# V loads of the eighteen late attention groups: from SyncE's queue to GpSimd's, in a planned attention and MLP kernel

## The chip, the cores and the metric

One core of a Trainium2 chip runs the program. The metric is the device time of one execution in microseconds, less is better. Engines are named as in the profile: PE is TensorE (PEld its weight loads), DVE VectorE, ACT ScalarE, POOL GpSimd, SP SyncE.

## What is computed

The reference is chunked attention with a few memory rows, then two MLPs in a row, all in float32:

```python
for c in range(nc):                      # 24 chunks of 32 queries; batch 4, heads 8, seq 768, head_dim 64
    q_c = q[:, :, c_start:c_end]
    k_full = np.concatenate([mem_k, k[:, :, l_start:r_end]], axis=2)   # 8 memory rows, 16 left, 32, 8 right
    v_full = np.concatenate([mem_v, v[:, :, l_start:r_end]], axis=2)
    scores = scale * np.matmul(q_c, k_full.transpose(0, 1, 3, 2))
    ...
    out[:, :, c_start:c_end] = np.matmul(a, v_full)                    # a: softmax of the scores
...
h = x @ w_in; g = s * np.maximum(h, 0) ** 2 + b; x = g @ w_out         # 3072 tokens, 512 -> 2048 -> 512
g = x @ w_gate; return (silu(g) * (x @ w_val)) @ w_out2                # 512 -> 1536 -> 512
```

## The kernel before

**Attention.** The 3072 queries are cut into 24 groups of 128 (four chunks, all eight heads), six groups to a batch. Three groups make a tile of 384 tokens, the unit of the first MLP. Groups 0 to 5 are called early (`EARLY`, L201): their work stands at the start of the program, and their queries and keys are turned by PE. Groups 6 to 23 are late: their work is spread among the first MLP's, and their queries and keys are loaded in blocks of 32 x 32 by `load_quadrant` (L312) into `qin` and `kin`, then turned by DVE: `turn_queries` writes `qt` (L355), `turn_keys` writes `kT` (L361). There is one `kin` and one `qt`, so the loads of a group can't start before `kT` of the group before it has been written. A late group has 36 such transfers, the first and the last of a batch 44. Below, K8 stands for the query and key transfers of group 8, kT8 and qt8 for its transposes, V8 for its values.

`load_values` (L377) fetches V of a group into one of two buffers by eight transfers, one for each chunk and half of the heads; at the ends of a sequence a chunk needs two pieces, and the first two groups of a batch load the memory rows too, and POOL copies these to the other three chunks (L391). So a group has 8, 10 or 12 transfers.

After the scores DVE takes the maximum (`mx`, L467), subtracts (`sc`, L480), sums (`rc`, L521, L524, L525) and, after the product with V, normalises (`on`, L530).

**First MLP.** Each weight pair (`load_w1`, L250; sixteen pairs, W0 to W15) is split by ACT and DVE into a high and a low part, so that three fast matmuls (L559, L560, L561) make one exact product; the last step of the split, L889, writes the low part. For a tile t and a slice m, `first_up` writes `hp` and `first_down` adds to `acc`. Between them DVE and ACT make `r`, its square, and the two parts `ghi` and `glo` (L612 or L610, L621 or L619). PE does the product up of the next slice before the product down of this one.

**Second MLP.** It begins at about 630 us and has no part in the change.

**What sets the order.** The program is not written in the order in which it runs. Every step is a task of a `Plan` (L63) with an engine, an estimated length, the tasks it depends on, and buffers that it takes and gives. `Plan.run` (L100) plays these tasks through in estimated time, always starting on a free engine the ready task with the longest way to the end, and the tasks are then emitted in the order in which they started there. PE's tasks are a fixed chain. DVE, ACT, POOL and SP each get one list, and on the chip each engine works through its list in order. A load is a task on SP, of 0.45 us per transfer, which needs one of two places called `fly`, followed by a task on MOVE, an engine that exists only in the plan:

```python
issue = issues[name] = plan.add(SP, 0.45 * n, emit, deps, [*get, "fly"], take=take)
return plan.add(MOVE, kilobytes / rate, None, [issue], put=["fly"], lag=1.8, give=give)
```

Of the kernel before, what the change touches and what calls it, by code (L numbers as in the profile page):

```python
# [146 lines left out]
def attention_and_two_mlps(  # L147
# [21 lines left out]
    nc = tc.nc  # L169
    B, H, S, D = q.shape  # L170
    NT, DM = out.shape
    NMEM = mem_k.shape[2]
# [7 lines left out]
    GB = S // GQ  # L180
    T = 3 * GQ
    NC = GQ // CHUNK
    WIN = LEFT + CHUNK + RIGHT
    KC = NMEM + WIN
# [16 lines left out]
    EARLY = 2 * GPB  # L201
# [110 lines left out]
    def load_quadrant(g, a, part):  # L312

        b, gi = divmod(g, GB)
        s0 = gi * GQ
        if a == 0 and part == 0:
            if "k" not in kept_in:
                kept_in["k"] = ld.tile([P, NP, KB, QUAD], F32, tag="kin", name="kin")
            loaded.setdefault(g, {})["q"] = ld.tile([P, NP, GQ // QUAD, QUAD], F32, tag="qin", name=f"qin{g}")
        e, half = divmod(a, 2)  # L320
        ds = slice(half * QUAD, (half + 1) * QUAD)
        qin, kin = loaded[g]["q"][a * QUAD:(a + 1) * QUAD], kept_in["k"][a * QUAD:(a + 1) * QUAD]

        def block(n, t, first, count):
            if count:
                nc.sync.dma_start(
                    out=kin[t:t + count, :, n], in_=k[b, e:H:2, first:first + count, ds].rearrange("j t i -> t j i")
                )

        at = s0 - LEFT  # L330
        left, over = max(0, -at), max(0, at + SPAN - S)
        whole = KB - 1 - (over > 0)
        if part == 0:
            if gi == 0:
                nc.sync.dma_start(out=kin[0:NMEM, :, 0], in_=mem_k[b, e:H:2, :, ds].rearrange("j t i -> t j i"))
            block(0, NMEM, 0, left)
            block(0, NMEM + left, at + left, QUAD - NMEM - left)
            if over:
                block(KB - 1, 0, S - QUAD + over, QUAD - over)
                block(KB - 1, QUAD - over, S - over, over)  # L340
            return
        for j in (2 * part - 2, 2 * part - 1):
            h = 2 * j + e
            first = at + QUAD - NMEM
            nc.sync.dma_start(
                out=kin[:, j, 1:1 + whole],
                in_=k[b, h, first:first + whole * QUAD, ds].rearrange("(n t) i -> t n i", t=QUAD),
            )
            nc.sync.dma_start(
                out=qin[:, j], in_=q[b, h, s0:s0 + GQ, ds].rearrange("(n t) i -> t n i", t=QUAD)  # L350
            )

    def turn_queries(g):
        staged[g] = {"qt": ap_.tile([P, NP, GQ], F32, tag="qt", name=f"qt{g}")}
        nc.vector.transpose(  # L355
            out=staged[g]["qt"].rearrange("p j s -> p (j s)"), in_=loaded[g]["q"].rearrange("p j n i -> p (j n i)")
        )

    def turn_keys(g):
        staged[g]["kT"] = t = ap_.tile([P, NP, KB * QUAD], F32, tag="kT", name=f"kT{g}")  # L360
        nc.vector.transpose(  # L361
            out=t.rearrange("p j s -> p (j s)"), in_=kept_in["k"].rearrange("p j n i -> p (j n i)")
        )

    def spread_keys(engine, g, mem):
        kT = staged[g]["kT"]
        if mem:
            copy(
                engine, staged[g]["kt"][:, :, :, 0:NMEM],
                kT[:, :, 0:NMEM].unsqueeze(2).to_broadcast([P, NP, NC, NMEM]),  # L370
            )
            return
        staged[g]["kt"] = kt = ap_.tile([P, NP, NC, KC], F32, tag="kt", name=f"kt{g}")
        w = kT[:, :, NMEM:KC]
        copy(engine, kt[:, :, :, NMEM:], bass.AP(tensor=w.tensor, offset=w.offset, ap=[w.ap[0], w.ap[1], [CHUNK, NC], [1, WIN]]))

    def load_values(g):  # L377

        b, gi = divmod(g, GB)
        s0 = gi * GQ  # L380
        n = g % 2
        if n not in v_bufs:
            v_bufs[n] = ld.tile([P, NC, NP, D], F32, tag=f"v{n}", name=f"v{n}")
        tv = v_bufs[n]
        for e in range(2):
            p0 = e * KC
            if gi < 2:
                mem = tv[p0:p0 + NMEM]
                nc.sync.dma_start(out=mem[:, 0], in_=mem_v[b, e:H:2].rearrange("h s d -> s h d"))
                for c in range(1, NC):  # L390
                    nc.gpsimd.tensor_copy(mem[:, c], mem[:, 0])  # L391
            for c in range(NC):
                a = s0 + c * CHUNK - LEFT
                left, over = max(0, -a), max(0, a + WIN - S)
                for row, first, n in (
                    (0, 0, left), (left, a + left, WIN - left - over), (WIN - over, S - over, over)
                ):
                    if n:
                        r0 = p0 + NMEM + row
                        nc.sync.dma_start(  # L400
                            out=tv[r0:r0 + n, c],
                            in_=v[b, e:H:2, first:first + n, :].rearrange("h s d -> s h d"),
                        )
        loaded.setdefault(g, {})["v"] = tv

    def bank(pool, tag, name):
# [2 lines left out]
    def stage_queries(g, early):  # L409
        tq = loaded[g]["q"]  # L410
        ps = bank(ps_acc, "acc2", f"psQ{g}") if early else bank(ps_a, "a", f"psQ{g}")
        qps = ps.rearrange("p (j s) -> p j s", j=NP)
        for j in range(NP):
            nc.tensor.transpose(qps[:, j, :], tq[:, j * P:(j + 1) * P], ident)
        staged[g] = {"q": qps}
# [370 lines left out]
    def second_store(h, s, i):  # L786
# [6 lines left out]
    ACT, DVE, PE, SP, MOVE = "ACT", "DVE", "PE", "SP", "MOVE"  # L793
    plan = Plan(
        dict(w=SLOTS - LENT, wt=SLOTS - 5, fly=2),
        dict(
            sc=LENT, f=2, own=1, qk=1, v=2, kT=1, kt=1, qt=1, at=1, on=1, x=2, r=4, ghi=2, glo=2, acc01=1,
            acc2=1, acc3=1, a=2, h=2, yq=1, so=1, a1=1, a2=1, a3=1, v1=2, v2=1,
        ),
    )  # L800
# [3 lines left out]
    def either(name, lengths, emit, *args, **kwargs):  # L804

        engine = list(lengths)[name in moved]
        return plan.add(engine, lengths[engine], lambda: emit(engine), *args, **kwargs)
# [3 lines left out]
    def transfer(deps, emit, n, kilobytes, get=(), take=(), give=(), rate=380.0, name=None):  # L811

        issue = issues[name] = plan.add(SP, 0.45 * n, emit, deps, [*get, "fly"], take=take)
        return plan.add(MOVE, kilobytes / rate, None, [issue], put=["fly"], lag=1.8, give=give)
# [96 lines left out]

    at_ = {}

    def plan_queries(g, early):
        vv = None
        if g >= EARLY:
            qk = None
            for a in range(12):
                qk = transfer(
                    [issues[f"K{g}_{a - 1}"]] if a else [], lambda a=a: load_quadrant(g, *divmod(a, 3)), 4 if a % 3 else 1,  # L920
                    64 if a % 3 else 14, take=["qk"] if a == 0 else (), rate=100.0, name=f"K{g}_{a}",
                )
                if a == 5:
                    vv = transfer([], lambda: load_values(g), 8, 460, take=["v"], rate=180.0, name=f"V{g}")
            t = plan.add(DVE, 0.60, lambda: turn_queries(g), [qk], take=["qt"])
            at_[g] = {"v": vv, "qt": t}
            t = plan.add(DVE, 0.72, lambda: turn_keys(g), [t], take=["kT"], give=["qk"])
            t = plan.add(ACT, 0.82, lambda: spread_keys(ACT, g, False), [t], take=["kt"])
            t = either(f"m{g}", {ACT: 0.26, DVE: 0.20}, lambda e: spread_keys(e, g, True), [t], give=["kT"])
            at_[g]["t"] = at_[g]["qt"], t  # L930
            return
        qk = transfer(
            [], lambda: load_tokens(g), 4, 590, take=["sc"], rate=180.0, name=f"K{g}"
        )
        vv = transfer([], lambda: load_values(g), 8, 460, take=["v"], rate=180.0, name=f"V{g}")
        at_[g] = {"v": vv, "qk": qk}
        t = plan.add(PE, 0.44, lambda: stage_queries(g, early), [qk], take=["acc2"] if early else ["a"])
        at_[g]["qt"] = either(
            f"q{g}", {ACT: 0.50, DVE: 0.60}, lambda e: stage_queries_copy(e, g), [t], take=["qt"],
            give=["acc2"] if early else ["a"],  # L940
        )
# [286 lines left out]
    for item in START.split():  # L1228
        what, g = item[0], int(item[1:] or 0)
# [105 lines left out]
```

## Time and profile before

| | us |
|---|---|
| median of three runs | 1224.76 (1222.81 to 1225.4) |
| the profiled execution's own time | 1225.08 |
| its span, first to last instruction | 1223.3 |
| PE busy | 1179.8 |
| DVE busy | 746.7 |
| POOL busy | 22.3 |

The profile shows one execution. PE busy for nearly the whole span does not mean that every stretch is alike: the stretches in which PE waits are the ones to look at, with what ended each wait. The trace has no group numbers; a group's `qt` row is found by counting: group 6 is the first transpose of L355, group 12 the seventh (271.89 us), group 18 the thirteenth (422.12 us). Times in microseconds are counted from the span's start.

### The profile page before, as it was taken

Reading aid. Unit: us, or ns where it says so; the run is one execution under the profiler, and the core shown is the slowest. Engines: PE = TensorE matmul, PEld = TensorE weight load, DVE = VectorE, ACT = ScalarE, POOL = GpSimd, SP = SyncE. Lnnn points to the kernel's source line nnn. Section 1 sums busy time; section 2 is a strip of 40 time slices with the busy share of each in tenths; the row PEclk is TensorE's granted clock in tenths of the full one; section 3 lists DMA queues with packets and bytes.
Section 4 is the critical chain, followed back from the end, with each engine's and each line's share of the span. In section 5 each row is a group of like instructions: output and inputs, shape, how many; then the busy total and the mean of one; then the engine's idle time right before and its main releaser. Section 6 shows DMA issues by size and latency. Waiting matters only on the chain.

```text
span 1223.3 us, 23310 instructions
## 1 busy us (share of the span) xinstructions
PE 1179.8 (96%) x9288; PEld 1119.8 (92%) x9288; DVE 746.7 (61%) x1306; ACT 481.8 (39%) x836; POOL 22.3 (2%) x54
## 2 busy tenths in 40 slices
PE   3788999999999999999999999999999999999998
PEld 3678999989999999999999899999999999999997
DVE  6899965556445444553387965578863357843343
ACT  2455433232333333333366544355532334432332
POOL 1001100001000000000000000000000000000000
PEclk9799999999999999999999999999999999999999
DMA  8857342223222222220247275296565296465251
GB/s 192 226 118 207 89 123 43 62 46 72 45 47 62 47 64 46 49 67 1 96 153 262 93 275 205 96 353 231 192 249 207 106 335 238 164 258 207 101 209 53
DMA packets 210203, 173.94 MB, mean 142 GB/s; under 512 B 157230, under 2 KB 182318, under 8 KB 209070
## 3 DMA queue, kind: packets, MB, share of 16 engines
q1 hardware_dynamic: 210094, 172.45, 44.7%
q8 instruction: 73, 1.20, 0.4%
q14 instruction: 36, 0.29, 0.1%
HBM read 124.40 MB, written 47.97 MB: 141 GB/s over the span
## 4 chain that ended last, share of the span: by engine, by line
PE 83%; DMA 5%; SPq 5%; DVE 4%; issue 1%; ACT 1%; DVEq 0%; ACTq 0%
PE acc L559 6%; PE acc L560 6%; PE acc L561 6%; PE hp L559 6%; PE chain_A L560 6%; PE chain_A L561 6%; PE oacc L561 6%; PE oacc L560 5%; PE chain_A L559 5%; PE hp L561 5%; PE hp L560 5%; PE oacc L559 5%; PE chain_B L559 4%; PE chain_B L560 4%; PE chain_B L561 4%; DMA raw_first<-in_moe_w_out_dram 2%
## 5 line engine op out<-in xcount | busy, mean ns | idle before, releaser
L559 PE MATMUL acc<-ghi,w_first 128*128 128x384 f32 x512 | 176.0, 344 | 2.4 <-DVE ghi L230 2.4
L560 PE MATMUL acc<-glo,w_first 128*128 128x384 f32 x512 | 173.3, 339 | 3.7 <-DVE glo L621 2.0
L559 PE MATMUL hp<-xhi,w_first 128*128 128x384 f32 x512 | 176.0, 344 | 0.7 <-ACT xhi L228 0.7
L560 PE MATMUL hp<-xlo,w_first 128*128 128x384 f32 x512 | 172.8, 338 | 1.1 <-DVE xlo L552 1.1
L561 PE MATMUL hp<-xhi,w_first 128*128 128x384 f32 x512 | 172.7, 337 | 0.0
L561 PE MATMUL acc<-ghi,w_first 128*128 128x384 f32 x512 | 172.5, 337 | 0.0
L729 ACT ACTIVATE kept<-chain_A 128x384 f32<-128x384 f32 x144 | 70.8, 492 | 185.1 <-PE chain_A L561 182.8
L560 PE MATMUL chain_A<-ops,hi_up 128*128 128x384 f32 x384 | 130.2, 339 | 0.0
L561 PE MATMUL chain_A<-ops,lo_up 128*128 128x384 f32 x384 | 129.5, 337 | 0.0
L559 PE MATMUL chain_A<-ops,hi_up 128*128 128x384 f32 x384 | 128.5, 335 | 0.0
L599 DVE SCALAR_TENSOR_TENSOR r<-r,s_sb 128x384 f32<-128x384 f32 x92 | 56.5, 614 | 110.0 <-ACT r L588 109.5
L588 ACT ACTIVATE r<-hp 128x384 f32<-128x384 f32 x96 | 47.0, 490 | 190.1 <-PE hp L561 185.4
L561 PE MATMUL oacc<-w_down,glo 128*128 128x512 f32 x288 | 114.6, 398 | 0.0
L560 PE MATMUL oacc<-w_down,ghi 128*128 128x512 f32 x288 | 114.0, 396 | 0.0
L559 PE MATMUL oacc<-w_down,ghi 128*128 128x512 f32 x288 | 112.1, 389 | 0.0
L560 PEld LDWEIGHTS acc<-glo,w_first 128*128 128x128 f32 x512 | 97.1, 190 | 6.3 <-DVE glo L619 3.3
L559 PEld LDWEIGHTS acc<-ghi,w_first 128*128 128x128 f32 x512 | 96.9, 189 | 4.7 <-DVE ghi L230 3.4
L559 PEld LDWEIGHTS hp<-xhi,w_first 128*128 128x128 f32 x512 | 97.3, 190 | 2.2 <-ACT xhi L228 0.9
L560 PEld LDWEIGHTS hp<-xlo,w_first 128*128 128x128 f32 x512 | 97.5, 190 | 1.3 <-DVE xlo L552 1.3
L561 PEld LDWEIGHTS hp<-xhi,w_first 128*128 128x128 f32 x512 | 97.2, 190 | 0.0
L561 PEld LDWEIGHTS acc<-ghi,w_first 128*128 128x128 f32 x512 | 97.0, 189 | 0.0
L734 DVE TENSOR_TENSOR kept<-chain_B,kept 128x384 f32<-128x384 f32 x48 | 26.7, 557 | 114.4 <-PE chain_B L561 114.4
(118 smaller groups left out, 2109.2 us busy)
## 6 DMA issues: line engine op xcount, KB each, us to landing
ops<-ops_dram SPq DMA_DIRECT2D x56, 768.0 KB
ops_dram<-ops SPq DMA_DIRECT2D x28, 768.0 KB
sum_dram<-o SPq DMA_DIRECT2D x48, 256.0 KB
v<-in_v_dram SPq DMA_DIRECT2D x176, 56.0 KB
raw_first<-in_moe_w_in_dram SPq DMA_DIRECT2D x16, 512.0 KB
raw_first<-in_moe_w_out_dram SPq DMA_DIRECT2D x16, 512.0 KB
o<-sum_dram SPq DMA_DIRECT2D x8, 1024.0 KB
y_dram<-y SPq DMA_DIRECT2D x32, 192.0 KB
```

The lines of the kernel that those rows point to most:

```text
L559: nc.tensor.matmul(o, whi, xhi, start=first, stop=False, skip_group_check=onto)
L560: nc.tensor.matmul(o, whi, xlo, start=False, stop=False, skip_group_check=onto)
L561: nc.tensor.matmul(o, wlo, xhi, start=False, stop=last, skip_group_check=onto)
L588: nc.scalar.activation(out=r, in_=hp, func=AF.Relu)
L599: nc.vector.scalar_tensor_tensor(out=r, in0=r, scalar=s_sb[:, 0:1], in1=r, op0=ALU.mult, op1=ALU.mult)
L729: nc.scalar.activation(out=t, in_=st2[n]["A"], func=AF.Copy)
L734: nc.vector.tensor_tensor(out=t, in0=st2[n]["B"], in1=kept, op=ALU.add)
```

## The change

```diff
     def load_values(g):
+        queue = nc.sync if g < EARLY else nc.gpsimd
...
-                nc.sync.dma_start(out=mem[:, 0], in_=mem_v[b, e:H:2].rearrange("h s d -> s h d"))
-                for c in range(1, NC):
-                    nc.gpsimd.tensor_copy(mem[:, c], mem[:, 0])
+                queue.dma_start(out=mem[:, 0], in_=mem_v[b, e:H:2].rearrange("h s d -> s h d"))
...
-                        nc.sync.dma_start(
+                        queue.dma_start(
                             out=tv[r0:r0 + n, c],
...
+        for e in range(2 if gi < 2 else 0):
+            mem = tv[e * KC:e * KC + NMEM]
+            for c in range(1, NC):
+                nc.gpsimd.tensor_copy(mem[:, c], mem[:, 0])
...
+    def load_v(g):
+        edge = 4 * (g % GB == 0) + 2 * (g % GB in (1, GB - 1))
+        issue = plan.add("POOL", 0.65 * (8 + edge), lambda: load_values(g), take=["v"])
+        return plan.add(MOVE, 0.15 * (8 + edge), None, [issue], lag=2.0)
...
                 if a == 5:
-                    vv = transfer([], lambda: load_values(g), 8, 460, take=["v"], rate=180.0, name=f"V{g}")
+                    vv = load_v(g)
```

V of groups 6 to 23 is issued by GpSimd, V of groups 0 to 5 by SyncE as before. In the plan the task moves from SP to POOL, and takes no place of `fly`. The copies of the memory rows, which POOL makes in both versions, now follow all of a group's transfers. Since the plan orders all engines by its own clock, the lists of DVE, ACT and SP change as well; PE's list is the same, row by row.

**SP at group 8.** W15 (`raw_first` in these rows) stands among K8's transfers, after 14 of 36 before. This is SP's list there, and at the end of K8, before:

```order
L326 DMA kin<-in_k_dram 24x4x32
L345 DMA kin<-in_k_dram 32x4x32
L349 DMA qin_1843<-in_q_dram 32x4x32
L345 DMA kin<-in_k_dram 32x4x32
L349 DMA qin_1843<-in_q_dram 32x4x32
L239 DMA raw_first_1924<-in_moe_w_in_dram 128x4x256
L244 DMA raw_first_1924<-in_moe_w_out_dram 128x1024
...
L345 DMA kin<-in_k_dram 32x4x32
L349 DMA qin_1843<-in_q_dram 32x4x32
L400 DMA v_155<-in_v_dram 56x4x64 x8
L648 DMA part<-part_dram 128x1536
L326 DMA kin<-in_k_dram 24x4x32
```

And now:

```order
L345 DMA kin<-in_k_dram 32x4x32
L349 DMA qin_1842<-in_q_dram 32x4x32
L239 DMA raw_first_1970<-in_moe_w_in_dram 128x4x256
L244 DMA raw_first_1970<-in_moe_w_out_dram 128x1024
L345 DMA kin<-in_k_dram 32x4x32
...
L345 DMA kin<-in_k_dram 32x4x32
L349 DMA qin_1842<-in_q_dram 32x4x32
L651 DMA part<-part_dram 128x1536
L326 DMA kin<-in_k_dram 24x4x32
```

The eight transfers of V8 are gone from SP's list, and W15 stands after 23 of K8's transfers instead of 14. DVE's list at the split of W15 (`t_first`, `raw_first`, `w_first`) and the normalisation of group 6 (`on`), before:

```order
L831 TENSOR_SCALAR t_first_1988<-t_first_1988 128x1024
L835 TENSOR_SCALAR t_first_1988<-t_first_1988 128x1024
L840 SCALAR_TENSOR_TENSOR raw_first_1924<-raw_first_1924,t_first_1988 128x1024
L599 SCALAR_TENSOR_TENSOR r<-r,s_sb 128x384
L847 SCALAR_TENSOR_TENSOR raw_first_1924<-raw_first_1924 128x1024
L530 TENSOR_TENSOR on_2073<-psV_0_2010,rc_1920 128x4x64
L530 TENSOR_TENSOR on_2073<-psV_1_2011,rc_1920 128x4x64
L621 SCALAR_TENSOR_TENSOR glo<-r,b_sb,ghi 128x384
L230 CAST w_first_2120<-raw_first_1924 128x1024
L599 SCALAR_TENSOR_TENSOR r<-r,s_sb 128x384
L889 TENSOR_TENSOR w_first_2120<-raw_first_1924,w_first_2120 128x1024
```

And now (line numbers from here on are three higher):

```order
L602 SCALAR_TENSOR_TENSOR r<-r,s_sb 128x384
L624 SCALAR_TENSOR_TENSOR glo<-r,b_sb,ghi 128x384
L533 TENSOR_TENSOR on_2063<-psV_0_2009,rc_1919 128x4x64
L533 TENSOR_TENSOR on_2063<-psV_1_2010,rc_1919 128x4x64
L834 TENSOR_SCALAR t_first_2074<-t_first_2074 128x1024
L838 TENSOR_SCALAR t_first_2074<-t_first_2074 128x1024
L843 SCALAR_TENSOR_TENSOR raw_first_1970<-raw_first_1970,t_first_2074 128x1024
L850 SCALAR_TENSOR_TENSOR raw_first_1970<-raw_first_1970 128x1024
L602 SCALAR_TENSOR_TENSOR r<-r,s_sb 128x384
L230 CAST w_first_2133<-raw_first_1970 128x1024
L470 TENSOR_REDUCE mx_2137<-psS_0_2080 128x4
L470 TENSOR_REDUCE mx_2137<-psS_1_2081 128x4
L892 TENSOR_TENSOR w_first_2133<-raw_first_1970,w_first_2133 128x1024
```

The normalisation now stands ahead of W15's steps, and the maxima of the next scores stand among them.

**DVE at group 12.** Its list there, before:

```order
L525 RECIPROCAL rc_3458<-rc_3458 128x8
L621 SCALAR_TENSOR_TENSOR glo<-r,b_sb,ghi 128x384
L590 TENSOR_SCALAR r<-hp 128x384
L355 STREAM_TRANSPOSE qt_3511<-qin_3197 128x512
L361 STREAM_TRANSPOSE kT_3518<-kin 128x640
L552 TENSOR_TENSOR xlo_3207<-psO_3500,xhi_3206 128x4x128
```

And now:

```order
L528 RECIPROCAL rc_3476<-rc_3476 128x8
L355 STREAM_TRANSPOSE qt_3498<-qin_3186 128x512
L624 SCALAR_TENSOR_TENSOR glo<-r,b_sb,ghi 128x384
L361 STREAM_TRANSPOSE kT_3502<-kin 128x640
L593 TENSOR_SCALAR r<-hp 128x384
L555 TENSOR_TENSOR xlo_3211<-psO_3504,xhi_3210 128x4x128
```

The transpose of the queries has moved ahead of `glo`, that of the keys ahead of `r`.

**DVE at group 18.** Its list there, before:

```order
L480 TENSOR_TENSOR sc_5439<-psB_1_5329,mx_5416 128x4x64
L599 SCALAR_TENSOR_TENSOR r<-r,s_sb 128x384
L521 TENSOR_REDUCE rc_5458<-sc_5439 128x8
L524 TENSOR_SCALAR rc_5458<-rc_5458 128x8
L525 RECIPROCAL rc_5458<-rc_5458 128x8
L355 STREAM_TRANSPOSE qt_5477<-qin_5162 128x512
L621 SCALAR_TENSOR_TENSOR glo<-r,b_sb,ghi 128x384
L361 STREAM_TRANSPOSE kT_5481<-kin 128x640
```

And now:

```order
L483 TENSOR_TENSOR sc_5439<-psB_1_5333,mx_5434 128x4x64
L355 STREAM_TRANSPOSE qt_5445<-qin_5134 128x512
L361 STREAM_TRANSPOSE kT_5453<-kin 128x640
L602 SCALAR_TENSOR_TENSOR r<-r,s_sb 128x384
L524 TENSOR_REDUCE rc_5479<-sc_5439 128x8
L527 TENSOR_SCALAR rc_5479<-rc_5479 128x8
L528 RECIPROCAL rc_5479<-rc_5479 128x8
L624 SCALAR_TENSOR_TENSOR glo<-r,b_sb,ghi 128x384
```

Both transposes now stand ahead of `r`, the three `rc` operations and `glo`; group 17's rows changed in the same way.

## Rows read from the trace of the kernel before

**Rows 1.** The page: span, then busy time, share of the span and instructions of each engine.

```profile
span 1223.3 us, 23310 instructions
PE 1179.8 (96%) x9288; PEld 1119.8 (92%) x9288; DVE 746.7 (61%) x1306; ACT 481.8 (39%) x836; POOL 22.3 (2%) x54
```

**Rows 2.** Windows: stretch, length, busy PE, PEld, DVE, ACT, POOL; PEclk, DMA share, GB/s.

```profile
90.00:120.00 30.00, 26.06 (x196) 24.09 (x195) 28.95 (x43) 17.13 (x25) 4.03 (x6) 0.94 0.66 196
...
150.00:180.00 30.00, 28.83 (x285) 27.80 (x285) 22.84 (x43) 8.70 (x15) 0.00 (x0) 1.00 0.47 125
180.00:270.00 90.00, 90.00 (x1002) 88.04 (x1001) 49.67 (x106) 29.73 (x51) 0.00 (x0) 1.00 0.25 49
270.00:300.00 30.00, 27.82 (x271) 26.72 (x270) 18.10 (x37) 6.41 (x11) 5.01 (x12) 0.94 0.29 55
```

**Rows 3.** Waits of PE, 262 to 300 and 415 to 450: total us, times, longest.

```profile
PE acc L559 <- DVE ghi L230: 2.0, 1, 2.0
PE acc L560 <- DVE glo L621: 2.0, 1, 2.0
```

**Rows 4.** DVE timeline: start, us, instruction [idle before it <- its end].

```profile
139.93 1.45 DVE L889 TENSOR_TENSOR w_first<-raw_first,w_first 128x1024 fp32r<-128x1024 f32 x1
...
165.79 1.22 DVE L889 TENSOR_TENSOR w_first<-raw_first,w_first 128x1024 fp32r<-128x1024 f32 x1
...
246.35 0.71 DVE L355 STREAM_TRANSPOSE qt<-qin 128x512 f32<-128x512 f32 x1 [2.25 <-DMA qin<-in_q_dram]
246.98 0.80 DVE L361 STREAM_TRANSPOSE kT<-kin 128x640 f32<-128x640 f32 x1
...
265.84 0.57 DVE L621 SCALAR_TENSOR_TENSOR glo<-r,b_sb,ghi 128x384 fp32r<-128x384 f32 x1
...
271.89 0.71 DVE L355 STREAM_TRANSPOSE qt<-qin 128x512 f32<-128x512 f32 x1 [3.70 <-DMA v<-in_mem_v_dram]
...
393.74 0.62 DVE L599 SCALAR_TENSOR_TENSOR r<-r,s_sb 128x384 f32<-128x384 f32 x1 [0.74 <-ACT r L588]
...
396.33 0.71 DVE L355 STREAM_TRANSPOSE qt<-qin 128x512 f32<-128x512 f32 x1 [0.94 <-DMA qin<-in_q_dram]
...
417.14 0.62 DVE L599 SCALAR_TENSOR_TENSOR r<-r,s_sb 128x384 f32<-128x384 f32 x1 [0.22 <-ACT r L588]
...
422.12 0.71 DVE L355 STREAM_TRANSPOSE qt<-qin 128x512 f32<-128x512 f32 x1 [3.32 <-DMA v<-in_mem_v_dram]
```

**Rows 5.** SP timeline: DMA issues.

```profile
144.47 0.30 SPq L326 DMA_DIRECT2D kin<-in_k_dram  x1
...
151.63 0.39 SPq L239 DMA_DIRECT2D raw_first<-in_moe_w_in_dram  x1
...
245.00 4.21 SPq L400 DMA_DIRECT2D v<-in_v_dram  x10
...
249.31 0.27 SPq L335 DMA_DIRECT2D kin<-in_mem_k_dram  x1
...
399.28 0.27 SPq L335 DMA_DIRECT2D kin<-in_mem_k_dram  x1
```

**Rows 6.** POOL timeline.

```profile
138.77 3.22 POOL L391 COPY v<-v 8x256 f32<-8x256 f32 x6 [25.07 <-DMA v<-in_mem_v_dram]
...
272.08 1.07 POOL L391 COPY v<-v 8x256 f32<-8x256 f32 x3 [130.10 <-DMA v<-in_mem_v_dram]
```

**Rows 7.** PE timeline.

```profile
167.60 0.33 PE L561 MATMUL hp<-xhi,w_first 128*128 128x384 f32 x1
...
268.04 0.34 PE L560 MATMUL acc<-glo,w_first 128*128 128x384 f32 x1
...
397.79 0.33 PE L560 MATMUL acc<-glo,w_first 128*128 128x384 f32 x1
...
423.39 0.45 PE L560 MATMUL acc<-glo,w_first 128*128 128x384 f32 x1 [2.03 <-DVE glo L621]
```

**Rows 8.** ACT timeline.

```profile
158.05 1.13 ACT L825 ACTIVATE t_first<-raw_first 128x1024 f32<-128x1024 f32 x1 [2.76 <-DMA qin<-in_q_dram]
```

## The prediction

> **What bounds the kernel now.** I read the span and the busy times first [rows 1]: TensorE (PE) works 1179.8 of 1223.3 us. So a change can gain only where PE waits, and the windows view says where that is [rows 2]. Between 180 and 270 us PE is busy for all 90 us, although attention runs there. It misses 3.94 us in 90 to 120, 1.17 in 150 to 180 and 2.18 in 270 to 300, where the mean granted clock is also down to 0.94 (a part of that stretch ran at the 1.2 GHz level; 0.06 of 30 us is 1.8 us of lost matmul time). VectorE (DVE) is busy 28.95 of 30 us in 90 to 120, and only 49.67 of 90 later. POOL does almost nothing: 22.3 us in all.
>
> Then I asked for PE's waits near the attention groups that begin a batch [rows 3]. Both are 2.0 us long and are ended by DVE writing a first-layer operand (ghi or glo), which has nothing to do with K, Q or V. The DVE timeline says why [rows 4]: DVE is an in-order queue, and the transpose of group 12's queries (271.89) stood 3.70 us waiting for its data, that of group 18 (422.12) 3.32 us. What PE needed was queued behind. So the loads' lateness reaches PE through DVE's queue. The SP timeline says why the loads are late [rows 5]: K and Q of a group are some 40 small transfers issued one after another, and they start only when kin is free, that is, after the preceding kT. For group 12 the first issue came at 249.31, after ten V transfers that held SP for 4.21 us from 245.00; kT of group 11 was done at 247.78 [rows 4], so V cost 1.5 us of start. The rest, 22.6 us from the first issue to the transpose, is K and Q alone.
>
> **The change, part by part.** *V off SP's queue.* SP loses 8 to 12 issues a group (4.21 us for ten [rows 5]). That is not a gain by itself: V is issued between the last K of a group and the next kT, where SP mostly waits anyway. It is worth at most the 1.5 us above, at the edges of a batch.
>
> *V on POOL's queue.* No row of before has a transfer issued by POOL. The nearest rows: a POOL copy takes 0.36 us (1.07 for three) with DVE waiting, 0.54 (3.22 for six) beside a busy DVE [rows 6]; an SP issue is 0.42 us (4.21 for ten). I take 0.5. Six groups carry 56 such transfers, and six groups last 150.2 us (from 271.89 to 422.12 [rows 4]), so POOL would be late only above 2.68 us each; two buffers for V leave a further group period of about 25 us. What hides it goes only there. Cost on the path: nothing.
>
> *The planner's new order on DVE.* The plan now believes that K arrives sooner, and hoists the transposes. At group 18 (and, by the same pattern, 17) they stood behind the first-layer r and the three rc operations; now they stand ahead of them. At group 12 qt now stands ahead of glo and r. So each edge has to be reckoned again, from the loads.
>
> Group 12: K11's data ended DVE's wait at 246.35; I let it come 0.8 earlier, since group 10's two transposes now follow each other, so 245.5. Transposes end 1.43 us later (246.35 to 247.78), K12 starts at once and needs its 22.6 us: 269.6. DVE gets to qt at 265.8, where glo now starts, and blocks for 3.8 us. Behind it comes glo, 0.70 + 0.57 us, done at 270.8. PE wanted it at 268.04 [rows 7]: a stall of 2.8 us where before it lost 2.2 (30 less 27.82 [rows 2]). **+0.6** (bounds: 0 if K11 gains another 0.6 at SP, +1.5 if it gains nothing).
>
> Group 17: qt waited until 396.33 at a place that DVE now reaches at 393.0 (before the gap of r at 393.74). With the start up to 1.4 earlier, qt comes at 394.9. Transposes 1.43, then r and the rc operations, 1.66 (417.14 to 418.80, where the gap before 422.12 begins), then glo 0.57: 398.5, while PE read glo at 397.79 [rows 7]. **+0.7** (0 to 2.1).
>
> Group 18: kT17 ends at 396.4; first issue to transpose took 422.12 - 399.28 = 22.84 [rows 4, 5], so qt at 419.2 and, with the same 3.66 us behind it, glo at 422.9. PE would have wanted it at 423.39 - 2.03 = 421.36 [rows 7], now 0.7 later for the stall of group 17, so it loses 0.8 instead of 2.03. **-1.2** (-2.0 to 0). The three together: **+0.1**. What SP gains, the hoisted transposes give back.
>
> *The last first-layer weight.* W15 stood behind 14 of group 8's 36 K and Q transfers, it now stands behind 23, because the plan thinks that K8 starts sooner. It can't start much sooner: kT7 frees kin, and DVE is full until then; the only help is that one weight operation (1.45 us, at 139.93 [rows 4]) now stands behind kT7, so K8 starts at 143.3 to 144.47. Fourteen transfers took 7.16 us (144.47 to 151.63 [rows 5]), 23 take 11.4 to 11.8, so W15 is issued at 154.7 to 156.2. Before, 6.42 us lay from that issue to ScalarE's first operation on it (158.05 [rows 8]), and 8.96 from there to the end of the last DVE step (165.79 + 1.22 [rows 4]). Between its steps stood two r, two normalisations and a glo; now one r and two maxima, of the size of the normalisations. That is an r and a glo less, 0.62 + 0.57, so 7.77. The end comes at 161.1 + 7.77 = 168.9 to 170.4, and PE, which before used wlo at 167.60 [rows 7] with 0.6 us to spare, waits for it. Against that, the normalisation no longer stands behind W15's steps, which ended PE's 1.1 us wait of 150 to 180. Without W15, PE would be there 1.1 earlier, so the bounds are -1.1 and +2.8; I take the early start, 168.9 - 167.6: **+1.3**.
>
> *DVE beside POOL.* Groups 6 and 7 bring 22 transfers (12 and 10) to POOL while DVE is full. A weight operation that ran beside POOL copies took 1.45 us instead of 1.22 [rows 4]; some 2.7 copies ran in that time, so 0.09 each. Bounds for a transfer: 0 (POOL waits, DVE doesn't) and 0.23. 22 x 0.09 is 2.0; the 1.05 us that DVE idles in 90 to 120 absorb half: **+0.9** (0 to 5.1). The twelve copies for the memory rows exist before and after.
>
> **Sum:** 0.1 + 1.3 + 0.9 = +2.3 us against the profiled execution's 1225.08 (1223.3 of span, 1.8 around it): 1227.4. That execution lies 0.3 above the median 1224.76; on the median's scale, **1227.0**. A measurement of this kernel tells 0.2%, 2.45 us, from no change; this is just inside it.
>
> **Rivals.**
> - *Slower: POOL's transfers hold DVE up.* For: DVE has hardly any slack in 90 to 120 us [rows 2], and the slowed operation above. Against: copies read SBUF for their whole length, an issue may not. It decides from about 0.15 us of DVE time a transfer; at 0.23 the term is 5.1 less 1.05, 3 us over the forecast: 1229 to 1232.
> The Trainium skill, SBUF — State Buffer, section Who interferes with whom, calls the pair of ports that DVE and GpSimd share an exclusive lock, held for a whole instruction by whoever comes first; by that rule either engine may pay, and the slowed row agrees that DVE does (1.45 against 1.22).
> - *Slower by far: POOL can't keep up.* Above 2.68 us a transfer V falls behind; at 3.0 us, 0.32 x 56 x 3 batches = 54 us, less 25 for the second buffer: about +29, 1254. Against: no row of POOL is above 0.54 us an instruction.
> The same page, section A bandwidth-pool intuition that's wrong, gives 0.62 us for a transfer issued by GpSimd alone and 3.1 beside a DVE copy. By the first the sum stands; by the second 56 transfers would need an estimated 174 us of the 150. No run here shows either, and late DVE work is mostly not copies.
> - *Faster: SP's relief counts.* If K lands about 3 us sooner than I reckon at groups 12, 17 and 18, the two stalls go (4.2 us), the clock's 1.8 with them, and 1.1 at 163 us: 1224.8 - 7.1 = 1217.7; half of it gives 1221. For: SP was late at exactly these places. Against: 22.6 us of issue for K12 contain no V.
> - *Nothing happens:* W15 in time and edges as before, 1224 to 1226; I count it to the forecast's own range, 1223 to 1230.
>
> **Chances.** Forecast with its own range 0.54 (0.36 within 0.2%, 0.18 slower); DVE held up 0.22; POOL too slow 0.04; SP's relief 0.20 (0.17 faster, 0.03 within). So faster 0.17, same 0.39, slower 0.44: cases of both signs are open, while the likeliest one is a small loss at the edge of what can be told. The range reaches down to 1221 and up to 1232, leaving out the best third of the relief, POOL too slow and the ends of the two slower cases.
>
> **What would show it.** In the profile after: no V row on SP; POOL rows for V at about 0.5 us; qt of groups 12 and 18 still preceded by DVE idle of 2 us or more, with PE waiting for glo right behind; a new short PE wait at about 398; PE waiting near 167 to 169 for the last DVE step of W15 and not for the normalisation; L889, L840 and casts before 120 us slightly longer. The prediction is wrong if PE's waits at 272 and 423 are gone (K came sooner than the issue rate allows), if W15 is not waited for, or if POOL's rows are over 2 us.

## The result, and the profile after

The changed kernel takes **1233.62 us** (median of 4, 1230.97 to 1235.31), the kernel before 1224.17 beside it: ratio 1.0081, 95% interval 1.0064 to 1.0097. The forecast was 1227.0, the range 1221 to 1232. The profiled execution took 1234.21.

From the page after: the span, busy times (us, share of the span, instructions), two DMA queues (packets, MB, share of the 16 DMA engines) and the group of V's transfers (busy, mean ns | idle before).

```profile
span 1232.4 us, 23323 instructions
...
PE 1177.9 (96%) x9288; PEld 1118.0 (91%) x9288; DVE 747.0 (61%) x1306; ACT 482.3 (39%) x836; POOL 127.5 (10%) x222
...
q1 hardware_dynamic: 175210, 164.09, 41.6%
q0 software_dynamic: 5376, 8.39, 2.8%
...
L399 POOL DMA_DIRECT2D v<-in_v_dram x156 | 99.2, 643 | 276.2 <-PE psB L513 198.8
```

PE is busy for 1177.9 us against 1179.8 [rows 1] and its mean granted clock is the same (0.990 against 0.989), so the 9.1 us more of span are waiting: PE is idle for 11.0 us more. V is on POOL at 643 ns a transfer, as the change says. The windows after, in the stretches of [rows 2] (busy us of each engine, then clock, DMA share, GB/s):

```profile
90.00:120.00 30.00, 21.56 (x166) 19.61 (x167) 23.08 (x34) 12.22 (x19) 10.17 (x18) 0.89 0.69 199
150.00:180.00 30.00, 26.46 (x258) 25.14 (x258) 23.35 (x41) 9.21 (x15) 5.25 (x8) 0.94 0.38 98
180.00:270.00 90.00, 90.00 (x1003) 88.05 (x1003) 49.47 (x101) 28.55 (x49) 17.45 (x28) 1.00 0.27 58
270.00:300.00 30.00, 26.40 (x265) 25.75 (x263) 14.66 (x30) 6.45 (x12) 8.58 (x18) 0.94 0.23 42
```

In 90 to 120 us PE loses 8.4 us where it lost 3.9 before, and DVE, which was full there, is idle for 7. In 150 to 180 PE loses 3.5 instead of 1.2. The new waits of PE (total us, times, longest) lie in 100 to 120 and in 155 to 180:

```profile
PE acc L562 <- ACT ghi L613: 5.1, 1, 5.1
...
PE hp L562 <- DVE w_first L230: 2.4, 1, 2.4
PE hp L564 <- DVE w_first L892: 1.2, 1, 1.2
```

The second pair of waits is that for W15, which was foreseen. The first was not: 5.1 us for a ghi of ScalarE. The timelines around it, POOL, SP, ACT, DVE and PE in this order:

```profile
94.33 0.57 POOL L390 DMA_DIRECT2D v<-in_mem_v_dram  x1 [3.28 <-issue]
94.89 2.58 POOL L399 DMA_DIRECT2D v<-in_v_dram  x4
97.47 0.79 POOL L390 DMA_DIRECT2D v<-in_mem_v_dram  x1
98.25 2.58 POOL L399 DMA_DIRECT2D v<-in_v_dram  x4
...
98.85 1.04 SPq L239 DMA_DIRECT2D raw_first<-in_moe_w_in_dram  x1
99.94 0.58 SPq L244 DMA_DIRECT2D raw_first<-in_moe_w_out_dram  x1
...
102.31 0.64 SPq L349 DMA_DIRECT2D qin<-in_q_dram  x1
...
107.48 1.12 ACT L828 ACTIVATE t_first<-raw_first 128x1024 f32<-128x1024 f32 x1 [7.16 <-DMA raw_first<-in_moe_w_out_dram]
...
110.11 0.95 ACT L228 ACTIVATE kt<-kT 128x896 f32<-128x896 f32 x1 [1.12 <-DVE kT L361]
110.96 0.60 ACT L613 ACTIVATE ghi<-r,b_sb 128x384 fp32r<-128x384 f32 x1
...
108.63 0.71 DVE L355 STREAM_TRANSPOSE qt<-qin 128x512 f32<-128x512 f32 x1 [6.49 <-DMA qin<-in_q_dram]
109.27 0.80 DVE L361 STREAM_TRANSPOSE kT<-kin 128x640 f32<-128x640 f32 x1
110.00 0.57 DVE L602 SCALAR_TENSOR_TENSOR r<-r,s_sb 128x384 f32<-128x384 f32 x1
...
111.61 0.69 PE L562 MATMUL acc<-ghi,w_first 128*128 128x384 f32 x1 [5.12 <-ACT ghi L613]
```

ScalarE stood 7.16 us for a weight pair (W10 in the plan's names) and DVE 6.49 us for group 6's queries. Behind these stood what PE needed: r, r on DVE, ghi. In the trace before, W10 (SP, then the first operation on it) stood so:

```profile
92.31 0.39 SPq L239 DMA_DIRECT2D raw_first<-in_moe_w_in_dram  x1
92.74 0.50 SPq L244 DMA_DIRECT2D raw_first<-in_moe_w_out_dram  x1
...
98.76 1.18 ACT L825 ACTIVATE t_first<-raw_first 128x1024 f32<-128x1024 f32 x1 [1.18 <-DMA raw_first<-in_moe_w_out_dram]
```

So W10 was in at 98.76 at the latest and is now in at 107.48. Two things have changed there: the plan puts it behind the four stores of part_dram, and V7 (V6 too, at 78.66 to 86) moves beside it on POOL's queue. Before, V6 and V7 stood in SP's queue behind W12.

### The profile page after: what moved, and what is told of

The parts are those of the page before. It is cut to its first block, busy times and chain, and to the rows that moved or that the text cites. A ratio compares the mean times of both kernels' runs of the same rounds, so it can differ in the third digit from the quotient of the medians.

```text
span 1232.4 us, 23323 instructions
## 1 busy us (share of the span) xinstructions
PE 1177.9 (96%) x9288; PEld 1118.0 (91%) x9288; DVE 747.0 (61%) x1306; ACT 482.3 (39%) x836; POOL 127.5 (10%) x222
## 3 DMA queue, kind: packets, MB, share of 16 engines
q1 hardware_dynamic: 175210, 164.09, 41.6%
q0 software_dynamic: 5376, 8.39, 2.8%
## 4 chain that ended last, share of the span: by engine, by line
PE 78%; SPq 9%; DMA 7%; DVE 4%; issue 2%; ACT 0%; DVEq 0%; ACTq 0%
PE chain_A L563 6%; PE chain_A L564 5%; PE oacc L564 5%; PE oacc L563 5%; PE chain_A L562 5%; PE oacc L562 5%; PE acc L562 5%; PE acc L563 5%; PE acc L564 5%; PE hp L562 5%; PE hp L564 5%; PE hp L563 5%; PE chain_B L562 4%; PE chain_B L563 4%; PE chain_B L564 4%; DMA raw_first<-in_moe_w_out_dram 4%
## 5 line engine op out<-in xcount | busy, mean ns | idle before, releaser
L399 POOL DMA_DIRECT2D v<-in_v_dram x156 | 99.2, 643 | 276.2 <-PE psB L513 198.8
```

The source lines that it names most:

```text
L399: queue.dma_start(out=tv[r0:r0 + n, c], in_=v[b, e:H:2, first:first + n, :].rearrange("h s d -> s h d"),)
```

## The experiments

**How the losses are placed.** PE's order of first-layer passes is the same in all kernels. In each trace I read the start of the first down product (acc<-ghi) of each of the 128 passes and subtract the start in the trace before. The lag of pass n is that difference. One execution each; up to pass 5 executions of one program differ by some us (the change and e5 are the same program up to there, -0.2 and +3.6), so what counts is the step from column to column. A profiled execution can also lie some us off its run's median, so the medians are compared too. The kernel before, run anew beside each set, had medians of 1225.59 us (e1 to e4), 1225.14 (e5 to e8) and 1224.97 (e9 to e11); each ratio is against the one of its set.

```
pass                5     6     8     9    19    21    41    43    72    73    74   127
before, us       90.9 103.6 112.8 117.6 165.0 173.5 267.8 280.8 416.4 420.9 427.5 666.2
the change       -0.2  -1.9  +5.4  +4.8  +2.4  +8.1  +8.0  +9.2  +9.4 +10.2  +8.4  +8.3
e1 queue only    +0.7  +1.2  +2.9  +4.4  +3.6  +3.5  +3.5  +0.8  +0.8  +0.8  -0.3  -0.4
e2 order only    +1.3  +2.9 +13.9 +13.3 +10.9 +16.4 +22.0 +23.2 +23.1 +24.5 +22.7 +22.6
e3 V6,V7 on SP   -0.4  +0.8  +1.6  +1.5  +1.6  +1.6  +1.5  +0.6  +2.0  +2.4  +0.6  +0.5
e4 late qt6      +0.4  +0.4  +4.8  +4.2  +1.7  +6.5  +6.4  +6.4  +7.4  +8.6  +7.0  +7.8
e5 early W15     +3.6  +3.3 +10.1  +9.5  +7.1  +9.4  +9.3  +8.0  +8.8  +9.5  +7.7  +7.6
e6 old plan, V8+ +1.2  +1.3  +1.2  +1.2  +1.7  +1.6  +1.6  -1.3  -0.9  -0.9  -2.3  -2.4
e7 no V6,V7      -0.3  -0.3  -0.3  -0.4  -2.5  +2.7  +2.6  +1.3  +3.2  +4.1  +2.4  +2.6
e8 e4, no V6,V7  +0.0  -0.1  -0.6  -1.2  -3.7  -0.3  -0.4  -0.9  -0.3  +0.8  -1.1  -0.4
e9 old plan,held +0.6  +0.8  +0.6  +0.6  +1.6  +1.6  +1.5  -1.0  -1.1  -1.1  -2.2  -2.3
e10 held, W15    -0.3  -0.6  +0.2  +0.2  -0.6  +1.7  +1.7  +2.9  +3.4  +4.5  +2.7  +2.6
e11 early W10    +0.2  +2.6  +3.5  +3.5  +2.4  +2.4  +2.4  +2.8  +3.3  +3.5  +1.7  +1.6
```

The change comes to pass 6 early by 1.9 us: its granted clock was 1.00 from 97 to 103 us, that of the kernel before 0.72. Then it loses 7.3 us between passes 6 and 8 (5.6 counted from pass 5), regains 3.0 up to pass 19, loses 5.7 at W15 (19 to 21), 1.2 at group 12 (41 to 43), 0.2 at group 17 (43 to 72) and wins 1.0 at group 18 (72 to 74).

**e1, the queue alone.** The kernel before with the load_values of the change; the plan is untouched (`transfer(...)` for V stays in it).

> The plan of the kernel before, V of the late groups issued by GpSimd: DVE, ScalarE, PE and the K and W transfers on SyncE stand as before. Order theory (the new plan puts qt and kT of group 6 in front of the glo of first-layer pass 7, and W15 late): no wait over 1 us at 103 to 113 us, time 1222 to 1226. Sharing theory (V6 and V7, moved by GpSimd while the weights load, make K6 and the weights late): PE waits 3 us or more at 103 to 113 us, 1228 or more. Port theory (GpSimd's transfers slow VectorE): no single wait, but DVE's instructions before 120 us are longer, 1226 to 1229.

Measured: 1223.98 us, ratio 0.998 (0.9969 to 0.9991). Two things in one: 3.2 us lost between passes 6 and 9 (a wait of 1.9 us for a ghi of DVE), and 3.8 won at groups 12 and 18. The wait lies between the signs of the two theories (none over 1 us, or 3 or more); the time is inside the order theory's range only because of the gain that neither had put there. The profiled execution, 1225.56, is among the longest of its ten.

**e2, the order alone.**

```diff
-        queue = nc.sync if g < EARLY else nc.gpsimd
+        queue = nc.sync
```

> The plan of the change, all V issued by SyncE at the places of that plan: PE, DVE and ScalarE stand as in the change. Order theory: the loss at 103 to 113 us stays (5 us or more against before) and so does the wait for W15, 1231 to 1240, since SyncE has the V transfers on top. Sharing theory: no loss over 2 us at 103 to 113 us, 1224 to 1229. Port theory: as the change less its 2 to 5 us, 1228 to 1231.

Measured: 1247.37 us, ratio 1.0178 (1.0163 to 1.0193), above the ranges of all three theories. SP now moves V6 and V7 where the new plan has them, ahead of W10: W10 is issued at 109.37, ScalarE waits 10.62 us for it and PE 7.04 for the ghi behind. It doesn't tell order from sharing, as I had thought, because V6 and V7 still go before W10, by another way. It does show that nothing special to GpSimd is needed for the loss.

**e3, V6 and V7 back on SP.**

```diff
-        queue = nc.sync if g < EARLY else nc.gpsimd
+        queue = nc.sync if g < EARLY + 2 else nc.gpsimd
...
-                    vv = load_v(g)
+                    vv = load_v(g) if g >= EARLY + 2 else transfer([], lambda: load_values(g), 8, 460, take=["v"], rate=180.0, name=f"V{g}")
```

> The change for groups 8 to 23 alone; V of groups 6 and 7 stays with SyncE, in plan and program. The plan then has qt of group 6 behind the glo of pass 7 and W15 behind 14 transfers of group 8, as before. All three theories: the loss before 170 us is gone; what remains is that of the edges at groups 12, 17 and 18, +0.1 by the prediction: 1223 to 1226. Above 1228 there is a further cost of GpSimd's transfers that none of them names.

Measured: 1227.86 us (1224.36 to 1230.26; the profiled execution 1225.62), ratio 1.002 (1.0009 to 1.0031). Both early losses are gone from the trace, as expected. The median is 1.9 us above the range; what the longer executions lose is not in this trace and stays open.

**e4, the transposes of group 6 back behind pass 7.**

```diff
+            turned[g] = t
...
+    plan.chain.append((g_ready[1, 1], turned[6]))
```

> The change, with one line of order more: the plan may not start qt of group 6 before the glo of pass 7; V6 and V7 are still moved by GpSimd. Order theory: PE's 5.1 us wait at 106 to 112 us falls to under 1.5 us, and 1225 to 1229 is left. Sharing theory: K6 and the weights still land at 107 us or later, the wait moves to a product that needs them and 4 us or more are still lost by 120 us, 1229 to 1234.

Measured: 1232.04 us, ratio 1.0051 (1.0036 to 1.0066). PE's one wait of 5.1 us becomes 1.8 for ghi and 1.3 for glo, and 4.4 us are still lost between passes 6 and 8. W10 comes in as late as before the repair (107.40, ScalarE idle for 4.83 us). How much the hoisted transposes cost isn't settled: 2.9 us by the step from pass 6 to 8, 0.6 by the lag at pass 8 (+4.8 against +5.4). The late data is the rest.

**e5, W15 early.**

```diff
+    plan.chain.append((issues["W15"], issues["K8_5"]))
```

> The change with the last first-layer weight pair (W15) behind 14 instead of 23 transfers of group 8, as before the change; DVE's order stays that of the change. If W15's late issue costs what the trace of the change shows (PE waits 3.6 us for its two last DVE steps, and runs at half clock behind that), the issue comes about 4.7 us earlier, both waits fall under 0.5 us, and the time is 1228 to 1231. If DVE's new order around those steps is what makes them late, the waits stay above 2 us, 1232 to 1235.

Measured: 1233.5 us (5 runs, 1228.6 to 1234.56), ratio 1.0055 (1.0034 to 1.0075). The waits are 0.5 and 1.2 us instead of 2.4 and 1.2; passes 19 to 21 lose 2.3 us instead of 5.7. W15's place is worth 3.4 us by the two traces; the medians don't tell e5 (1.0055) from the change (1.0081, intervals that overlap). The median is 2.5 us above the expected range: the profiled execution (1233.5) was 3.6 us late by pass 5 already, where the program is still that of the change. Where the 1.2 us that stay come from, no run shows: between the two last steps stood an r of 0.61 us before, and now two maxima of 0.75 together.

**e6, the old plan with V of groups 8 to 23 on GpSimd.** As e1, but `queue = nc.sync if g < EARLY + 2 else nc.gpsimd`.

> The plan of the kernel before, V of groups 8 to 23 issued by GpSimd, V of groups 6 and 7 by SyncE as before. From the run with all late V on GpSimd under this plan: it lost 2.8 us against before at 103 to 117 us and won 3.9 us at 272 and 423 us. If the loss came of V6 and V7 moving beside the weights, it goes and the gain stays: 1219.5 to 1222.5. If the gain at 272 and 423 us depended on the shift before it, 1223 to 1226.

Measured: **1222.51 us**, ratio 0.9973 (0.996 to 0.9985). It beats both kernels, the one before by 2.6 us. The loss of e1 is gone (+1.3 to +1.2), the gain is there: -2.9 at group 12, -1.4 at group 18.

**e7, the change without V6 and V7.** Their 22 transfers and 12 copies are left out; every other instruction stands where the change has it.

> The change without the 22 transfers and 12 copies of V of groups 6 and 7 (these groups use the V that stands in the buffers); order of all else unchanged. Sharing theory: K6 and the weights land earlier, the loss between 103 and 113 us falls from 7.4 to under 4 us, 1228 to 1231. Order theory alone: K6 and the weights land as late as in the change because SyncE issues them late, the loss stays at 6 to 7.4 us, 1232 to 1235.

Measured: 1231.28 us, ratio 1.0052 (1.0032 to 1.0072). The loss between passes 6 and 8 is not under 4 us but gone: -0.3 to -0.3. By the medians less comes back than by the traces: the time over the kernel before falls from 9.45 to 6.14 us, while the lag at pass 127 falls from 8.3 to 2.6; the profiled execution, 1228.52, is the shortest of its four. ScalarE (W10) and DVE (qt of group 6) in this trace:

```profile
103.32 1.13 ACT L828 ACTIVATE t_first<-raw_first 128x1024 f32<-128x1024 f32 x1 [1.42 <-DMA raw_first<-in_moe_w_out_dram]
...
104.18 0.71 DVE L355 STREAM_TRANSPOSE qt<-qin 128x512 f32<-128x512 f32 x1 [0.51 <-DMA qin<-in_q_dram]
```

W10 is in 4.2 us earlier than in the change, qt 4.5 earlier, with the same order. Half of W10's 4.2 us is its issue (97.82 instead of 99.94, SP's queue having been slowed from V6 on), half the way from issue to use. The DMA queues in 95 to 108 us say the same (packets, MB, share): before, then the change, then e7.

```profile
q1 hardware_dynamic: 3470, 4.55, 104.9%
```

```profile
q1 hardware_dynamic: 3036, 2.61, 70.8%
q0 software_dynamic: 320, 0.48, 15.4%
```

```profile
q1 hardware_dynamic: 3431, 3.96, 94.3%
```

With V7 in the second queue the two together bring 3.09 MB in these 13 us, without it SP's queue alone brings 3.96. Later issue has a part in this: the four weight pairs from W10 on are issued 1.53 to 4.25 us earlier in e7. Before that, in 86 to 90 us, the 16 DMA engines are busy for 0.95 of the time in the change and for 0.28 in e7.

**e8, e4 without V6 and V7.**

> The kernel with qt of group 6 behind the glo of pass 7 (which lost 4.5 us at 103 to 113 us against before) without the 22 transfers and 12 copies of V of groups 6 and 7. Sharing theory: the loss there falls under 1.5 us, 1226 to 1229. If it is the order of the weight pairs on SyncE that is left, 3 us or more stay, 1230 to 1232.

Measured: 1229.28 us (1225.36 to 1234.64), ratio 1.0031 (1.0016 to 1.0047). Between passes 6 and 8 it gains 0.5 us, where e4 lost 4.4: sharing, not the order of the weight pairs. The median is just above the sharing theory's range; the profiled execution, 1225.5, is among its shortest, so what the longer ones lose stays open.

**e9, the old plan, V6 and V7 held.** As e1, with one copy more ahead of V6 on GpSimd:

```diff
+        if g == EARLY:
+            last = raw1[list(raw1)[-1]]
+            nc.gpsimd.tensor_copy(tv[0:1, 0, 0, 0:1], last[0:1, 1, 0:1].bitcast(F32))
```

> The plan of the kernel before, all late V issued by GpSimd, but GpSimd first copies one element of the last weight pair issued ahead (W12), so that V6 and V7 are moved only when that pair is in. If what the first run under this plan lost (2.8 us by 113 us, 3.6 by 117) came of the time at which V6 and V7 move, it goes: under 1 us is lost there and the time is 1220 to 1223, as with V6 and V7 on SyncE. If it came of the queue that moves them, wherever it stands, 2 us or more stay, 1223 to 1226.

Measured: 1224.37 us, ratio 0.9991 (0.9978 to 1.0004); by its trace 0.2 us gained instead of e1's 1.7 lost between passes 6 and 8, and the gain of e6 behind it. GpSimd now starts V6 at 113.47. By these traces it is the time at which V6 and V7 move, not the queue. The medians don't show it: 0.9991 is told neither from no change nor from e1's 0.998, and 1224.37 lies 1.4 us above its expectation. The clean test is e10.

**e10, the change repaired at both places.** GpSimd's V6 and V7 stand behind the same copy, put into its queue when W12 is issued, and W15 is chained as in e5. PE, DVE and ScalarE have the order of the change, instruction for instruction, and SP's list is that of e5.

> The change, with the order of PE, DVE and ScalarE untouched, and two repairs: V6 and V7 start only when weight pair W12 is in, and W15 stands behind 14 instead of 23 transfers of group 8. If the late V6 and V7 and the late W15 are the two losses, PE's 5.1 us wait at 106 us and its 3.6 us at 170 us both go, the loss by 113 us is under 1.5 us, and 1224 to 1228 is left. If the new order of DVE and ScalarE costs by itself, 3 us or more stay lost by 113 us, 1229 or more.

Measured: 1227.53 us, ratio 1.0018 (1.0002 to 1.0034). Between passes 6 and 8 it loses 0.8 us instead of 7.3, at W15 2.3 instead of 5.7. The rest is the edges: +1.2, +0.5 and -0.7. Against e5 only the time at which V6 and V7 move is different, on the same queue and in the same order of all else: 2.6 us over the kernel before instead of 8.4, with intervals that meet only at 1.0034. So the time at which these 22 transfers move is shown as a cause by the medians too.

**e11, W10 early.**

```diff
+    plan.chain.append((issues["W10"], part_stored[0].deps[0]))
```

> The change with one demand on the plan: weight pair W10 is issued ahead of the four stores of the first-layer partial sums, as before the change. The plan then takes back by itself nearly all its new order up to 170 us (qt of group 6 behind the glo of pass 7, W15 behind 14 transfers of group 8); V6 and V7 still move by GpSimd at 79 to 103 us. If the place of W10 is the lever of the whole loss, what is left by 117 us is what the first run lost there, 2 to 4 us, no wait for W15 stands, and the time is 1225 to 1229. If GpSimd's V6 and V7 alone make the loss, 5 us or more stay by 117 us, 1230 or more.

Measured: 1230.42 us (1227.15 to 1231.52; profiled 1227.43), ratio 1.0043 (1.0028 to 1.0059). This one demand brings back the old order up to 170 us: no wait for W15, and +3.5 at pass 9, as expected. But the time is 1.4 us above its range, and behind V7's transfers PE has lost 2.4 us at pass 6 already (2.2 for a ghi, which stood on DVE behind W10's first step; that came at 104.29). It doesn't decide how much of the rest is W10's place.

## Why the prediction was wrong, step by step

**V on POOL's queue: "Cost on the path: nothing". This is the step that failed.** I priced POOL's time alone. That was right: 643 ns against 0.5 assumed, far under 2.68. But a transfer also has a time at which it moves its bytes, and a queue of its own changes it. In SP's queue V6 and V7 stood behind W10 to W12; on POOL they go as soon as their buffers are free, at 79 to 103 us, into the stretch where weight pairs and group 6's last transfers are what PE waits for next. Without them the lag at pass 8 is 5.7 us smaller (e7), with them held until the weights are in, 5.2 smaller (e10). The order alone does nothing there (e10: +0.8), the transfers alone 1.7 to 3.2 (e1), both together 7.3 (5.6 from pass 5): the new plan brings W10 in 4.6 us later (98.76 to 103.32, e7) and puts the transposes ahead of glo, which uses up the slack, and the transfers add 4.2. Behind PE's wait of 5.12 us the granted clock is down too: 0.50, the 1.2 GHz level, from 110 to 115 us.

The Trainium skill has the rule that I should have weighed (DMA: Bandwidth & Descriptors, section Issuing engines are not separate DMA queues): transfers of all issuing engines run on the same 16 DMA engines and interleave, and to spread them saves only the time of issue. The trace agrees as to the sharing: SP's queue brings 2.61 MB in 95 to 108 us beside V7 and 3.96 without it, the later issue included. As to the gain, e6 shows what saved issue time is worth here: 2.6 us.

**DVE beside POOL: +0.9, and the rival built on it.** Hardly anything. Two of DVE's operations on the weights (count | total us, mean ns) in 78 to 104 us, the change first, then e7, which has none of these transfers:

```profile
L850 DVE SCALAR_TENSOR_TENSOR raw_first<-raw_first 128x1024 uint32<-128x1024 uint32 x3 | 3.6, 1217 | 0.0
L892 DVE TENSOR_TENSOR w_first<-raw_first,w_first 128x1024 fp32r<-128x1024 f32 x3 | 3.6, 1217 | 0.0
```

```profile
L892 DVE TENSOR_TENSOR w_first<-raw_first,w_first 128x1024 fp32r<-128x1024 f32 x3 | 3.6, 1218 | 0.0
L850 DVE SCALAR_TENSOR_TENSOR raw_first<-raw_first 128x1024 uint32<-128x1024 uint32 x3 | 3.6, 1217 | 0.0
```

Two steps beside V6's transfers did take longer, a cast of w_first at 82.14 and L838 at 84.66: 0.87 us each against 0.68 in e7. That is 0.4 us of the 2.0 that I had put there before slack, and the lag at pass 5 behind them is that of e7 (-0.2 and -0.3). So the rival with the right sign had the wrong mechanism. POOL doesn't wait either: DVE was busy through 94 to 100 us, and four transfers took 2.58 us there, 0.645 each, as the mean of all 156 (0.643). The Trainium skill (SBUF — State Buffer, section A bandwidth-pool intuition that's wrong) gives 0.62 us for a transfer issued by GpSimd alone, with which this agrees, and 3.1 beside a DVE copy, which no row here shows (POOL's longest transfer of V in the change is 0.79).

**W15: +1.3.** Right in place and mechanism, but too small: the 4.1 measured lie outside its bounds of -1.1 and +2.8. In e7, where nothing comes before it, W15 was issued at 154.81 (I said 154.7 to 156.2) and its last DVE step ended at 168.50 (168.9 to 170.4). But PE came there 2.5 us ahead of the kernel before (pass 19), where I had counted 1.1, and waited for two steps, 1.9 and 1.2 us. Left out was also the clock behind the wait: 0.64 in 168 to 172 us of that trace, 1.4 us. In the change group 7's transposes came 3.9 us later than before (145.2 against 141.3), W15 was done 5.4 us later than in e7 (173.93), and PE by then was only 2.4 behind the kernel before: the lag grew by 4.1 in all (+4.0 at pass 17 to +8.1 at pass 21).

**The edges: +0.1.** Measured +1.2, +0.2, -1.0, together +0.4, where I had +0.6, +0.7, -1.2. The wait behind qt of group 12 is there, longer than the 2.8 I had reckoned (DVE, then PE):

```profile
278.58 0.71 DVE L355 STREAM_TRANSPOSE qt<-qin 128x512 f32<-128x512 f32 x1 [4.61 <-DMA qin<-in_q_dram]
...
279.84 0.54 PE L563 MATMUL acc<-glo,w_first 128*128 128x384 f32 x1 [3.60 <-DVE glo L624]
```

"What SP gains, the hoisted transposes give back" was right, and the runs show both halves: with the old order (e6) SP's relief wins 2.9 us at group 12 and 1.4 at group 18. The relief is the start, which I had put at 1.5 us at most, not a faster K: K12 is first issued 0.03 us after kT11 has ended (249.31), where it was 1.5 before, and K18 likewise (397.51), where it was 1.0; K12 still needs 22.8 us from there. The shorter wait also leaves the granted clock at 1.00 in 270 to 280 us, where it was 0.83 before: 1.7 us, which I had counted to the rival alone. At group 12 the wait of 2.0 us [rows 3] is down to 0.6 (waits of e6 in 262 to 300 us):

```profile
PE acc L562 <- DVE ghi L230: 0.6, 1, 0.6
```

In the change itself the wait at group 18 is down to 0.5 us, behind 1.78 us of idle DVE where I wanted 2 or more: by the prediction's own list half a sign that it was wrong there. So the faster rival was real, at 4.3 of its 7.1 us by the trace of e6 and 2.6 by the medians, and it was the new plan that spent most of it.

**The sum.** Predicted 0.1 + 1.3 + 0.9 = 2.3. Measured by passes: 0.4 at the edges, 4.1 at W15, nothing to be seen for DVE, and for the term that was missing 7.3, less the 1.9 us by which pass 6 came early; 1.4 came back up to pass 17 (+5.4 to +4.0). That makes the +8.3 at pass 127.

## What to carry to other kernels

Taking a load off a shared queue also takes away its place behind the loads that were ahead of it. Before moving it, list what else is moving at the time at which its buffer comes free, and who waits for that; if that is the critical data, hold the load or move only those that have no such company, as e10 and e6 do. And when a planner sets the order, test the queue under the old plan and the new plan under the old queue: here the one was a gain of 0.2% (e1) and the other a loss of 1.8% (e2).

## What was not expected of the hardware

V through GpSimd's queue goes in other packets: 8.39 MB in 5376 (1.56 KB each), while the packets of SP's queue fell from 210094 to 175210, that is by 34884 for the same bytes (240 B each).

POOL's copies can pay more than the 0.23 us that a step of DVE does [rows 4]: six copies of V's memory rows took 4.65 us in e9 beside a full DVE (121.31 to 125.96), 0.78 each, against 0.36 [rows 6]. The prediction has the 0.36 with DVE waiting, and that was misread: from 272.08 to 273.15 us DVE was at the transposes of group 12 (qt at 271.89, then kT until 273.3). So a busy DVE alone doesn't make a copy slow; which of its operations do, no run here separates.
